# A 40-row product split over the two halves of TensorE's rows, in a linear-attention and mixture-of-experts kernel

## Chip, cores and metric

The kernel runs on one core of one Trainium2 chip, in fp32 (matmuls of the second part in fp32r). The metric is the time of one execution in device microseconds (us), as the core's own clock gives it. Full-speed TensorE clock is written 1.00; the profile shows which share of it was granted.

## What is computed

The first part is a recurrence over 768 tokens for 4 batches and 8 heads of width 40; its output feeds a mixture of 8 experts whose gate is normalized in 8 rounds over rows and columns.

```python
for t in range(S):                       # S = 768, state is [B, H, 40, 40]
    y[:, :, t] = einsum('bhd,bhde->bhe', rt, state)
    Sa = einsum('bhde,bhe->bhd', state, at)
    state_decay = state * wt[:, :, None, :] - einsum('bhd,bhe->bhde', Sa, bt)
    state = state_decay + einsum('bhd,bhe->bhde', vt, kt)
...
P = exp(logits - logits.max())           # logits = x @ w_gate, x = y as [3072, 320]
for _ in range(8):
    P /= P.sum(1, keepdims=True) + 1e-09
    P /= P.sum(0, keepdims=True) + 1e-09
    P *= N / E
for e in range(E):
    out += P[:, e:e + 1] * (maximum(x @ w1[e], 0.0) @ w2[e])
```

## The kernel before

**The recurrence in chunks.** The tokens are cut into 12 chunks of 64, and each chunk of each batch is one unit, 48 in all. A unit holds four pairs of heads (p, `NP` = 4). Of a pair, one head lies on partitions 0 to 39 and the other on 64 to 103 (`R2` = 104 rows); the rows between are padding. Three kinds of work make up the first part:

- **Preparations** (`prep`, 48 of them, numbered cb). One loads `inp` by DMA, forms the running products of the decays by two scans on VectorE (`q`, L124, and `g`, L134), scales k and b by `q` into `kb` (L147) and a by `g` into `ab` (L153, L154), and multiplies the two on TensorE into `ll` (L159): for each pair one product with the 128 columns of `kb` as weights. `ab` is laid out with 128 columns, of which the first head fills 0 to 63 in its rows and the second 64 to 127 in its own; the other two blocks were set to zero once at the start (L85), so that one product over all 104 rows gives both heads side by side. Then `kb` is transposed into `kt` (L167). `ll` goes to `sx` (VectorE, L169, with a mask) and to `lt` (ScalarE, L161 or L173), from which a DMA takes it to `ld` in DRAM; `kt` goes to `sx` and `bb` by three copies on ScalarE (L174 to L176). The first six preparations (`NFAST`) scale `ab` on VectorE, the others on GpSimd.
- **Inversions**: for every two chunks a triangular system is loaded back from `ld` (`load_lu`) and inverted in small steps on VectorE (L184 to L207), then assembled on TensorE and ScalarE (`tmat`: `gp`, L261, and `op`, L266, with weights of 64 rows by 64 columns).
- **Recurrence steps** (`recur`): `av`, `xc`, `pu`, `c2` and `zt` on TensorE, with evacuations on VectorE and ScalarE, and `y` (L321) and `z` (L330) on GpSimd. Spread between them are the gate's small products `lp` (L345).

**Buffers.** PSUM has eight banks: four for the recurrence steps (pool `ps`), two in pool `pq` and two in pool `pt`. `pq` holds `ll`, one bank each, and from preparation 6 on (`NKB` = 6) also `kt`; `pt` holds `gp`, `op`, `lp`, and `kt` of the first six. `kb`, `lt` and `q` have one buffer from preparation 6 on, `inp`, `g` and `ab` two.

**Order.** Events are sorted by hand-given times (`ev`), and a scheduler then places each engine's instructions by its own model of their lengths. Each engine works its queue in order. The second part (the experts, from L582 and L647) is dense TensorE work and follows the first.

## Time and profile before

| | us |
|---|---|
| median of 3 runs | 1834.67 (1831.1 to 1841.27) |
| the profiled execution | 1832.94, its span 1831.2 |
| TensorE busy over the span | 1724.3 (94%) |
| VectorE, ScalarE, GpSimd busy | 1365.3, 856.8, 874.0 |
| first and last `ll` product | 10.4 and 367.9 |
| last `op` product of the first part | 489.7 |

The first row is what a comparison goes by; the second is the execution whose trace is read here. Busy time of TensorE is counted from an instruction's start to its modelled end, and instructions overlap, so that 94% does not mean that no more would fit. The first part fills the first 500 us; all that the change touches lies in the first 371 us.

### The profile page before, as it was taken

Reading aid. Unit: us, or ns where it says so; the run is one execution under the profiler, and the core shown is the slowest. Engines: PE = TensorE matmul, PEld = TensorE weight load, DVE = VectorE, ACT = ScalarE, POOL = GpSimd, SP = SyncE. Lnnn points to the kernel's source line nnn. Section 1 sums busy time; section 2 is a strip of 40 time slices with the busy share of each in tenths; the row PEclk is TensorE's granted clock in tenths of the full one; section 3 lists DMA queues with packets and bytes.
Section 4 is the critical chain, followed back from the end, with each engine's and each line's share of the span. In section 5 each row is a group of like instructions: output and inputs, shape, how many; then the busy total and the mean of one; then the engine's idle time right before and its main releaser. Section 6 shows DMA issues by size and latency. Waiting matters only on the chain.

```text
span 1831.2 us, 31655 instructions
## 1 busy us (share of the span) xinstructions
PE 1724.3 (94%) x11843; PEld 1696.8 (93%) x11843; DVE 1365.3 (75%) x2356; ACT 856.8 (47%) x1851; POOL 874.0 (48%) x854
## 2 busy tenths in 40 slices
PE   4479988999989999999999999999999999999999
PEld 4368888898978999999999999999999999999999
DVE  7786996973788867777676878977686877767675
ACT  6347767766743533434343434345343343424342
POOL 6545664723462626447291735008182644628160
PEclk8568988999999999999999999999999999999999
DMA  7468777867520101111020112201020111102001
GB/s 193 116 157 185 175 180 174 186 137 172 152 77 20 57 20 57 38 39 57 20 75 20 57 37 61 69 1 60 16 76 20 57 38 38 57 20 75 15 24 44
DMA packets 211759, 140.47 MB, mean 77 GB/s; under 512 B 162965, under 2 KB 193813, under 8 KB 211605
## 3 DMA queue, kind: packets, MB, share of 16 engines
q1 hardware_dynamic: 207925, 132.70, 27.9%
q10 hardware_dynamic: 3680, 5.74, 1.2%
q8 instruction: 94, 1.54, 0.3%
q14 instruction: 60, 0.49, 0.1%
HBM read 110.78 MB, written 27.61 MB: 76 GB/s over the span
## 4 chain that ended last, share of the span: by engine, by line
PE 75%; DVE 7%; DMA 4%; issue 4%; POOL 3%; ACT 2%; SPq 2%; POOLq 0%; ACTq 0%; DVEq 0%
PE op L647 36%; PE p L582 33%; DMA inp<-in_inp_dram 1%; PE xc L297 1%; PE av L289 1%; PE pu L308 1%; DVE pr L193 1%; DVE hl L606 1%; DVE q L124 1%; PE c L315 1%; DMA ld<-lt 1%; PE op L266 1%; DVE sm L600 1%; PE ll L159 1%; POOL ab L154 1%
## 5 line engine op out<-in xcount | busy, mean ns | idle before, releaser
L582 PE MATMUL p<-xch,wh 128*128 128x384 f32 (+1 forms) x1792 | 605.0, 339 | 8.9 <-DVE sm L600 4.3
L603 ACT ACTIVATE hh<-sm 128x384 fp32r<-128x384 f32 x512 | 269.5, 527 | 728.5 <-DVE sm L600 728.4
L647 PE MATMUL op<-wh,hh 128*128 128x320 f32 x1536 | 477.2, 311 | 4.0 <-ACT hh L603 3.8
L647 PE MATMUL op<-wl,hh 128*128 128x320 f32 x1536 | 474.8, 310 | 0.0
L647 PE MATMUL op<-wh,hl 128*128 128x320 f32 x1536 | 468.0, 309 | 0.9 <-DVE hl L606 0.9
L528 POOL TENSOR_TENSOR wl<-ws,wh 128x640 fp32r<-128x640 f32 x60 | 103.1, 1718 | 606.2 <-ACT wh L526 606.1
L606 DVE SCALAR_TENSOR_TENSOR hl<-sm,hh 128x384 fp32r<-128x384 f32 x512 | 373.1, 762 | 2.6 <-ACT hh L603 1.8
L582 PEld LDWEIGHTS p<-xch,wh 128*128 128x128 f32 (+1 forms) x1792 | 337.0, 188 | 13.3 <-DVE sm L600 5.2
L582 PE MATMUL p<-xcl,wh 128*128 128x384 f32 x896 | 302.3, 337 | 0.0
L582 PE MATMUL p<-xch,wl 128*128 128x384 f32 x896 | 301.8, 337 | 0.0
L647 PEld LDWEIGHTS op<-wh,hh 128*128 128x128 f32 x1536 | 290.2, 189 | 4.9 <-ACT hh L603 4.9
L647 PEld LDWEIGHTS op<-wl,hh 128*128 128x128 f32 x1536 | 291.1, 190 | 0.0
L647 PEld LDWEIGHTS op<-wh,hl 128*128 128x128 f32 x1536 | 286.8, 188 | 1.4 <-DVE hl L606 1.2
L600 DVE TENSOR_TENSOR sm<-p,u 128x384 f32<-128x384 f32 x384 | 236.3, 625 | 8.7
L582 PEld LDWEIGHTS p<-xcl,wh 128*128 128x128 f32 x896 | 168.6, 188 | 0.0
L582 PEld LDWEIGHTS p<-xch,wl 128*128 128x128 f32 x896 | 168.5, 188 | 0.0
L600 DVE TENSOR_TENSOR sm<-p,p 128x384 f32<-128x384 f32 x128 | 71.3, 557 | 129.4 <-PE p L582 75.0
L600 DVE TENSOR_TENSOR p<-p,p 128x384 f32<-128x384 f32 x128 | 71.1, 556 | 101.7 <-PE p L582 101.4
L600 DVE TENSOR_TENSOR u<-p,p 128x384 f32<-128x384 f32 x128 | 70.8, 553 | 57.1 <-PE p L582 55.9
L536 POOL TENSOR_TENSOR wl<-ss,wh 128x512 fp32r<-128x512 f32 x60 | 90.3, 1505 | 28.4 <-ACT wh L533 24.2
L159 PE MATMUL ll<-ab,kb 104*128 104x128 f32 x336 | 62.8, 344 | 40.5 <-POOL kb L147 18.5
L159 PEld LDWEIGHTS ll<-ab,kb 104*128 104x128 f32 x336 | 54.2, 244 | 45.3 <-POOL kb L147 24.8
(163 smaller groups left out, 2727.3 us busy)
## 6 DMA issues: line engine op xcount, KB each, us to landing
ws<-in_wts_dram SPq DMA_DIRECT2D x60, 832.0 KB, 4.5
inp<-in_inp_dram SPq DMA_DIRECT2D x42, 451.5 KB, 4.5
gd<-g SPq DMA_DIRECT2D x48, 113.8 KB, 2.6
gl<-gd SPq DMA_DIRECT2D x48, 113.8 KB, 2.8
vz<-in_v_dram SPq DMA_DIRECT2D x48, 112.0 KB, 3.5
xd<-y SPq DMA_DIRECT2D x24, 224.0 KB, 3.5
ld<-lt ACTq DMA_DIRECT2D x40, 128.0 KB, 2.6
rb<-in_r_dram SPq DMA_DIRECT2D x96, 48.0 KB, 3.1
```

Of the source, the lines that this page charges most:

```text
L124: nc.vector.tensor_tensor_scan(out=qr.rearrange("r p t -> r (p t)"), data0=w65[:, 260:0:-1], data1=one65, initial=0.0, op0=ALU.mult, op1=A ...
L154: eng.tensor_tensor(out=ab[64:104, :, 64:128], in0=a_in[64:104], in1=g[64:104], op=ALU.mult)
L159: nc.tensor.matmul(ll[:, p], lhsT=kb[:, p], rhs=ab[:, p], start=True, stop=True)
L193: nc.vector.tensor_tensor(out=prv, in0=a.unsqueeze(2).broadcast_to([nu, n_c, n_r, n_k]), in1=m.unsqueeze(1).broadcast_to([nu, n_c, n_r, n_ ...
L266: nc.tensor.matmul(op[:, p], lhsT=gs[:, p], rhs=t2[:, p], start=True, stop=True)
L528: g.tensor_tensor(out=wl[:, 0:640], in0=raw[:, 256:896], in1=wh[:, 0:640], op=ALU.subtract)
L536: g.tensor_tensor(out=lv[:, 3:7], in0=so[:, :, 0], in1=hv[:, 3:7, 0], op=ALU.subtract)
L582: nc.tensor.matmul(o, lhsT=w_, rhs=x_, start=(j == 0), stop=(j == 3))
L600: eng.tensor_tensor(out=out, in0=x, in1=y, op=ALU.add)
L603: nc.scalar.activation(out=hh[:, f, h], in_=sm[f][:, h], func=AF.Relu)
L606: v.scalar_tensor_tensor(out=hl[:, f, h], in0=sm[f][:, h], scalar=0.0, in1=hh[:, f, h], op0=ALU.max, op1=ALU.subtract)
L647: nc.tensor.matmul(ops[i], lhsT=a[:, h, cs], rhs=w_[:, cw], start=(f == 0 and h == 0 and j == 0), stop=(last and h == 1 and j == 2))
```

## The change

The product of a preparation is taken for each head by itself: weights are the 40 rows of that head, moving data the 64 columns of its `ab`, so that the heads at rows 0 and 64 use different halves of TensorE's rows (two row tiles of 64). They write into different banks: `ll` is now one buffer of two banks, heads in one bank each, and `pq` has one such buffer (`PQ` = 1). `ab` loses its zero blocks and is filled by one operation over 104 rows in place of two over 40. `kt` of all preparations is now in `pt`.

```diff
-    ab_b = [pin.tile([R2, NP, 128], F32, name=f"ab{i}") for i in range(2)]
+    ab_b = [pin.tile([R2, NP, 64], F32, name=f"ab{i}") for i in range(2)]
...
-    for t in g1_b + ab_b:
+    for t in g1_b:
         nc.vector.memset(t, 0.0)
...
-        eng.tensor_tensor(out=ab[0:40, :, 0:64], in0=a_in[0:40], in1=g[0:40], op=ALU.mult)
-        eng.tensor_tensor(out=ab[64:104, :, 64:128], in0=a_in[64:104], in1=g[64:104], op=ALU.mult)
-        nc.scalar.copy(out=sx[64:104, :, 0, 0:64], in_=ab[0:40, :, 0:64])
-        nc.scalar.copy(out=sx[64:104, :, 1, 0:64], in_=ab[64:104, :, 64:128])
-        ll = pq.tile([128, NP, 2, 64], F32, name="ll", tag="pq")
+        eng.tensor_tensor(out=ab, in0=a_in[0:R2], in1=g[0:R2], op=ALU.mult)
+        nc.scalar.copy(out=sx[64:104, :, 0, 0:64], in_=ab[0:40])
+        nc.scalar.copy(out=sx[64:104, :, 1, 0:64], in_=ab[64:104])
+        lb = pq.tile([128, 2, 512], F32, name="ll", tag="pq")
         for p in range(NP):
-            nc.tensor.matmul(ll[:, p], lhsT=kb[:, p], rhs=ab[:, p], start=True, stop=True)
+            for h in range(2):
+                r = slice(h * 64, h * 64 + 40)
+                nc.tensor.matmul(lb[:, h, p * 64:p * 64 + 64], lhsT=kb[r, p].rearrange("r k t -> r (k t)"),
+                                 rhs=ab[r, p], start=True, stop=True)
+        ll = lb[:, :, 0:256].rearrange("x h (p t) -> x p h t", p=NP)
...
-            kt = pt.tile([128, NP, 2, 64], F32, name="kt", tag="pt")
-        else:
-            kt = pq.tile([128, NP, 2, 64], F32, name="kt", tag="pq")
+        kt = pt.tile([128, NP, 2, 64], F32, name="kt", tag="pt")
...
-PQ = 2
+PQ = 1
```

Lines below the edit stand one further down in the changed kernel (L167 becomes L168). The scheduler places the work anew. Three places show it. The first is TensorE's queue where the first inverse is assembled (`gp`, `op`), behind the preparations of the second group. Before:

```order
L159 MATMUL ll_1100<-ab1_222,kb_1090 128x128 x4
L167 MATMUL kt_1105<-cst_162,kb_1090 128x104 x4
L261 MATMUL gp_934<-td_219,lg_220 64x32 x8
L266 MATMUL op_945<-td_219,lg_220 64x32 x8
L261 MATMUL gp_1059<-td_219,lg_220 64x32 x8
L308 MATMUL pu_985<-x1_966,tt0_217 128x104 x4
```

In the changed kernel:

```order
L160 MATMUL ll_885<-ab1_222,kb_876 128x64 x8
L262 MATMUL gp_980<-td_219,lg_220 64x32 x8
L160 MATMUL ll_1059<-ab0_221,kb_1050 128x64 x8
L267 MATMUL op_991<-td_219,lg_220 64x32 x8
L168 MATMUL kt_1068<-cst_162,kb_1050 128x104 x4
L309 MATMUL pu_1031<-x1_1012,tt0_217 128x104 x4
```

A preparation's `ll` now stands between `gp` and `op`, its `kt` behind `op`, and the second `gp` comes after the next recurrence products; `kt`, `gp` and `op` draw on the same two banks.

The second place is GpSimd's queue in the preparations of the second group (the numbers name buffers). Before:

```order
L147 TENSOR_TENSOR kb_499<-st15_191,q_492 104x512
L152 COPY cc8_184<-q_581 104x4
L153 TENSOR_TENSOR ab0_221<-inp_579,g_584 40x4x64
L154 TENSOR_TENSOR ab0_221<-inp_579,g_584 40x4x64
L147 TENSOR_TENSOR kb_588<-inp_579,q_581 104x512
```

In the changed kernel:

```order
L147 TENSOR_TENSOR kb_518<-st15_191,q_511 104x512
L152 COPY cc8_184<-q_603 104x4
L153 TENSOR_TENSOR ab0_221<-inp_601,g_606 104x256
L147 TENSOR_TENSOR kb_610<-inp_601,q_603 104x512
```

One operation on `ab` stands between two on `kb`, in the same order otherwise.

The third place is VectorE's queue in the first 45 us, where `ll` of the first preparations is taken out of PSUM into `sx` (the buffer numbers are left out of `q` and `ll`). Before:

```order
L169 TENSOR_TENSOR sx_164<-ll,cst 64x8x64
L134 SCALAR_TENSOR_TENSOR g<-inp,g_223 112x260
L124 SCALAR_TENSOR_TENSOR q<-st_192,cst 112x260
L153 TENSOR_TENSOR ab_222<-inp,g 40x4x64
L154 TENSOR_TENSOR ab_222<-inp,g 40x4x64
L128 RECIPROCAL g_223<-q 112x4
L134 SCALAR_TENSOR_TENSOR g<-st_192,g_223 112x260
L169 TENSOR_TENSOR sx_167<-ll,cst 64x8x64
```

In the changed kernel:

```order
L170 TENSOR_TENSOR sx_164<-ll,cst 64x8x64
L128 RECIPROCAL g_223<-q 112x4
L153 TENSOR_TENSOR ab_222<-inp,g 104x256
L134 SCALAR_TENSOR_TENSOR g<-st_191,g_223 112x260
L170 TENSOR_TENSOR sx_167<-ll,cst 64x8x64
L170 TENSOR_TENSOR sx_170<-ll,cst 64x8x64
L170 TENSOR_TENSOR sx_173<-ll,cst 64x8x64
L170 TENSOR_TENSOR sx_176<-ll,cst 64x8x64
```

The scans of the two preparations that follow have moved ahead of `sx_164`, and four masks of `ll` stand together, each of which now empties the only `ll` buffer before the next product may start.

## Prediction

> **What bounds the kernel now.** I read three views, in this order: busy time by stage, the chain of work that ended last, and single rows of the timeline. First the stages (columns: stretch, its length, busy us of TensorE, its weight loads, VectorE, ScalarE and GpSimd with counts, granted clock, DMA share, GB/s).

> ```profile
> 0.00:57.00 57.00, 28.94 (x142) 25.57 (x143) 38.17 (x67) 34.24 (x84) 38.07 (x66) 0.76 0.72 177
> 57.00:107.00 50.00, 21.66 (x96) 19.11 (x95) 42.92 (x71) 18.92 (x48) 29.97 (x32) 0.50 0.53 132
> 107.00:380.00 273.00, 245.63 (x2274) 235.38 (x2274) 215.72 (x379) 188.60 (x477) 150.76 (x176) 0.90 0.79 176
> 380.00:500.00 120.00, 114.99 (x1120) 109.99 (x1119) 74.95 (x136) 79.31 (x188) 43.88 (x53) 0.96 0.67 157
> 500.00:1831.00 1331.00, 1313.06 (x8217) 1306.75 (x8215) 993.58 (x1705) 535.70 (x1055) 611.28 (x528) 1.00 0.13 43
> ```

> From 500 us on TensorE is full (1313 of 1331 us) and nothing there is edited. Preparations run in the first three stretches. Up to 107 us no engine is full and TensorE runs at half clock for much of it; from 107 to 380 us TensorE is busy for 90%, VectorE for 79%. Which of them ends last is said by the chain of waits from 57 to 380 us, by line:

> ```profile
> by line: issue 16.9%; DMA inp<-in_inp_dram 8.0%; DVE pr L193 4.8%; DVE q L124 3.9%; DMA ld<-lt 3.9%; PE ll L159 3.8%; POOL ab L154 3.5%; POOL ab L153 3.2%; DMA lu<-ld 3.2%; POOL kb L147 3.0%; DVE gt L196 2.9%; DVE g L134 2.9%; POOL y L321 2
> ```

> It is spread thin: the loads of `inp`, the scans, the inversion and GpSimd's scaling all take turns. The two `ab` operations hold 6.7% of 323 us, 21.6 us; the product `ll` 3.8%, 12.3 us. These are the two terms that the change can move most.

> **The product on two halves.** How one instruction follows the next on TensorE at full clock (columns: start, length to the last modelled end, what, count; every fp32 product is recorded twice):

> ```profile
> 228.71 1.63 PE L297 MATMUL xc<-f,st 104*104 104x104 f32 x16
> 236.19 1.08 PE L159 MATMUL ll<-ab,kb 104*128 104x128 f32 x8
> 237.11 0.52 PE L167 MATMUL kt<-cst,kb 104*128 104x104 f32 x4
> 239.79 0.98 PE L345 MATMUL lp<-gs,y 104*128 104x8 f32 x8
> 240.63 1.14 PE L159 MATMUL ll<-ab,kb 104*128 104x128 f32 x8
> ```

> `ll` holds TensorE from 236.19 to the start of `kt` at 237.11: 0.92 us for 8 records, 0.115 each. `lp` has the same 128 weight columns but 8 moving columns instead of 128, and takes 0.84 for 8 records. So it is the weights that set the pace, and halving the moving columns gains nothing by itself. [...]

> The new product has 16 records with 128 weight columns each. All then hangs on whether the halves work side by side. The trace has one place where products on rows 0 to 63 (`gp`) and on rows 64 to 127 (`op`) wait in the queue together, at half clock:

> ```profile
> 110.40 1.91 PE L261 MATMUL gp<-td,lg 64*64 64x32 f32 x16 [0.73 <-DMA td<-nd]
> 114.25 1.59 PE L266 MATMUL op<-td,lg 64*64 64x32 f32 x13 [1.95 <-ACT lg L263]
> 115.56 0.31 PE L261 MATMUL gp<-td,lg 64*64 64x32 f32 x1
> 115.67 0.29 PE L266 MATMUL op<-td,lg 64*64 64x32 f32 x1
> 115.69 0.29 PE L261 MATMUL gp<-td,lg 64*64 64x32 f32 x1
> 115.77 0.29 PE L266 MATMUL op<-td,lg 64*64 64x32 f32 x1
> 115.80 0.29 PE L261 MATMUL gp<-td,lg 64*64 64x32 f32 x1
> ```

> Alone, `gp` goes at (1.91 - 0.29) / 15 = 0.108 us a record. Interleaved, `gp` still steps by 0.11 (115.69 to 115.80) and `op` by 0.10 (115.67 to 115.77): each half keeps its own pace. So eight records per half beside each other: 8 x 0.115 = 0.92 us. The densest row of records bounds how fast 16 can be issued:

> ```profile
> 230.08 0.26 PE L297 MATMUL xc<-f,st 104*104 104x104 f32 x1
> 230.27 0.30 PE L261 MATMUL gp<-td,lg 64*64 64x32 f32 x2
> 230.50 1.12 PE L289 MATMUL av<-rb,vz 104*104 104x128 f32 x8
> 234.70 1.11 PE L266 MATMUL op<-td,lg 64*64 64x32 f32 x16
> ```

> `op` goes at (1.11 - 0.22) / 15 = 0.059 (0.22 is the length of one), and 16 x 0.059 = 0.94 us. I take 0.94; the upper end is 16 x 0.115 = 1.84, the lower 0.92. The same rows price a change of tile size. `xc` steps by (1.63 - 0.26) / 15 = 0.09, but from its last record to `gp` it is 0.19: 0.10 more. The two `gp` records need 0.12, but `av` starts 0.23 later: 0.11 more. Together 0.21 us for going in and out, 0.4 at half clock. [...]

> So a preparation costs TensorE 0.94 + 0.21 - 0.92 = 0.23 us more at full clock, about 0.4 at half. For 31 preparations after 107 us that is 7.1 us, for the 8 from 57 to 107 us 3.2, in all 10.3. `ll` is busy for 56.9 us in this stretch (rows below) and 12.3 of them lie on the chain, a fifth; TensorE's queue is dense, so that a delay also pushes what is behind it. I take a third: **+3.4 us** (0 to +10.3).

> **One operation for `ab`.** Groups of the two stretches (busy us, mean ns, then idle time before and its releasers); the first two rows are those of 57 to 107 us, the others of 107 to 380:

> ```profile
> L159 PE MATMUL ll<-ab,kb 104*128 104x128 f32 x64 | 16.8, 441 | 28.3 <-POOL kb L147 15.5 <-POOL ab L154 12.8
> L154 POOL TENSOR_TENSOR ab<-inp,g 40x256 f32<-40x256 f32 x8 | 7.8, 972 | 0.6
> ...
> L159 PE MATMUL ll<-ab,kb 104*128 104x128 f32 x248 | 40.1, 310 | 6.9 <-POOL ab L154 4.6 <-POOL kb L147 2.2
> L147 POOL TENSOR_TENSOR kb<-inp,q 104x512 f32<-104x512 f32 x30 | 37.7, 1257 | 45.1 <-DVE q L124 30.6 <-PE kt L167 7.1 <-PE xc L297 6.1
> L154 POOL TENSOR_TENSOR ab<-inp,g 40x256 f32<-40x256 f32 x30 | 29.0, 968 | 2.3
> L153 POOL TENSOR_TENSOR ab<-inp,g 40x256 f32<-40x256 f32 x30 | 24.3, 809 | 21.5 <-DVE g L134 12.5 <-ACT c L304 2.5 <-ACT bb L176 2.4
> L124 DVE TENSOR_TENSOR_SCAN q<-inp,cst 112x260 f32<-112x260 f32 x30 | 24.1, 802 | 21.4 <-DMA inp<-in_inp_dram 17.5 <-POOL kb L147 3.1 <-POOL ab L154 0.7
> L321 POOL TENSOR_TENSOR y<-ws,gl 104x256 f32<-104x256 f32 x28 | 23.6, 842 | 29.9 <-DVE ws L317 27.2 <-issue 1.7 <-DVE g L128 0.2
> ```

> The pair costs (24.3 + 29.0) / 30 = 1.78 us. The one that takes its place has the shape of `y`, 104x256, which takes 0.84 in the same stretch: GpSimd's time follows the 256 elements of a row, not the rows. That saves 0.94 of 1.78, so at most 21.6 x 0.94 / 1.78 = 11.4 us of the chain. What is late next stands in the same rows: `kb` has waited 30.6 us for VectorE's `q`, and `q` 17.5 us for the load of `inp`, which an `ab` that is done sooner does not shorten where `kb` frees the buffer last. I take half: **-5.7 us** (0 to -11.4).

> **The start, to 57 us.** Gone are the zero blocks; and six `ab` pairs are single operations on VectorE:

> ```profile
> 1.19 1.03 DVE L85 MEMSET ab<- 104x512 f32 x2
> L153 DVE TENSOR_TENSOR ab<-st,g x4: 402/411/418, 9.4 to 26.8; 40x256 f32<-40x256 f32 x4
> L154 DVE TENSOR_TENSOR ab<-st,g x4: 423/423/1293, 9.9 to 27.2; 40x256 f32<-40x256 f32 x4
> L154 DVE TENSOR_TENSOR ab<-inp,g x2: 1295/1296/1296, 30.7 to 35.0; 40x256 f32<-40x256 f32 x2
> ```

> That is 1.03 us of memsets and six second operations of 0.42 to 1.30, 4.3 us with the medians; VectorE is busy for 38.2 of 57 us, so a part of the 5.3 shows: -1.5, between 0 and -5. Against it stands the single `ll` buffer: a product now waits for the mask of the one before. Such a turn is about 2.1 us of product at half clock and 0.7 of mask, and the four masks in a row make four turns; with two buffers product and mask overlapped by up to 0.7. I take +1.5 (0 to +4). Together **0** (-5 to +4).

> **`kt` in `pt`.** No row of before shows the 42 later `kt` beside `gp`, `op` and `lp`. Nearest is how long one holds its bank:

> ```profile
> 180.94 0.52 PE L167 MATMUL kt<-cst,kb 104*128 104x104 f32 x4
> 181.83 0.42 ACT L174 COPY sx<-kt 64x320 f32<-64x320 f32 x1
> 182.57 0.30 ACT L176 ACTIVATE bb<-kt 64x160 f32<-64x160 f32 x1
> ```

> From 180.94 to 182.87, 1.9 us; 31 of them hold 60 of the 546 bank-us of two banks in 273 us. That is little, but what waits for a bank waits at the head of TensorE's queue, and recurrence products stand behind it. If a quarter of each hold is waited for, 0.5 x 31 = 16 us. Below nothing: `ll` and `kt` no longer take turns in one pool, worth up to -2. I take **+2** (-2 to +16).

> **Sum**: +3.4 - 5.7 + 0 + 2 = -0.3 us on the profiled execution's 1832.9, so 1832.6; its own range, with the terms half way to their ends, 1825 to 1840. The profiled execution lies 1.7 us under the median of the three runs, inside their scatter. About 0.5%, 9 us, is what a measurement of this kernel can tell from no change.

> **Rivals.** *Faster, the shorter `ab` counts in full.* The chain gives the whole 11.4, the start 5, the extra time on TensorE hides in the 10% that it idles before 380 us: 1832.9 - 16.4 = 1816.5. For it: `ll` waited 28.3 us in 57 to 107 us, 12.8 of it for `ab`. Against: `q` and the loads are close behind. Chance 0.24. *Slower, the banks of `pt`.* `gp`, `op`, `lp` and `kt` wait for each other's evacuation at the head of TensorE's queue, 0.5 us per preparation: 1832.9 + 3.4 - 5.7 + 16 = 1846.6. It decides from 0.37 us per preparation on (31 x 0.37 = 11.5, which with the other terms is +9). For it: `ll` now stands between `gp` and `op`, with `kt` behind. Against: 60 of 546 bank-us. Chance 0.18. *The halves work in turn*, so that the change does not do what it says: 1.84 + 0.21 - 0.92 = 1.13 us more per preparation, 35 us for 31, and 2.1 at half clock, 17 for 8. Half of these 52, with -5.7 and +2: 1855. The interleaved rows speak against it; they have 64 weight columns, not 128. Chance 0.08.

> **How the numbers follow.** The forecast has 0.50, of which I give 0.04 to each side for the scheduler's new placement. Faster by over 0.5%: 0.24 + 0.04 = 0.28; slower: 0.18 + 0.08 + 0.04 = 0.30; within: 0.42. The range takes in the fast rival and the bank rival and leaves out most of the third: 1815 to 1851.

> **What would show it.** Records of `ll` that alternate between the halves about 0.06 us apart, and some 0.94 us from the first `ll` record to `kt`'s, plus a gap of 0.1 on either side: the product's term. One `ab` row of about 0.84 us on GpSimd, and `ab` under 12 us on the chain: the second. Rows of `gp`, `op`, `lp` or `kt` that wait for ScalarE's copies out of a `pt` bank: the fourth; more than 12 us of these and the forecast is wrong. `ll` of 2 us at full clock would prove the halves in turn.

## The result and the profile after

| kernel | median us | ratio to before, 95% interval |
|---|---|---|
| before | 1836.1 (1831.1 to 1841.27, 4 runs) | |
| changed | 1901.71 (1897.6 to 1906.08, 4 runs) | 1.0357 (1.0318 to 1.0397) |

The change costs 3.6%, some 66 us; the forecast was 1832.6 us, with a range that ended at 1851. The profiled execution took 1906.08 us, its span is 1904.2, 73.0 more than the span of the execution profiled before (each profile shows one execution, so this distance is not exactly that of the medians). Its stages, in the columns of the prediction's first view:

```profile
57.00:107.00 50.00, 21.17 (x150) 17.79 (x148) 39.92 (x68) 17.92 (x45) 18.22 (x23) 1.00 0.52 134
107.00:430.00 323.00, 289.56 (x2382) 272.00 (x2383) 215.07 (x373) 182.73 (x460) 114.74 (x145) 0.76 0.67 149
430.00:570.00 140.00, 135.09 (x1264) 129.08 (x1262) 75.96 (x142) 87.83 (x211) 44.05 (x56) 0.90 0.61 140
570.00:1904.00 1334.00, 1317.22 (x8233) 1311.53 (x8233) 990.50 (x1707) 536.44 (x1057) 610.97 (x528) 0.99 0.13 43
```

The same stretch of the kernel before:

```profile
107.00:430.00 323.00, 294.70 (x2770) 281.75 (x2771) 254.66 (x446) 219.48 (x556) 161.75 (x193) 0.91 0.77 171
```

The last stage does the work that filled 500 to 1831 us before, with TensorE busy for 1317 us against 1313, so almost nothing was lost there. In 323 us from 107 on TensorE issued 2382 records against 2770, and every engine and the DMA did less: less work got done, on a TensorE that was busy all the same, at a granted clock of 0.76 instead of 0.91. The 0.76 is too high and the 1.00 up to 107 us says nothing, since the trace after has no clock entry before 127 us and such a stretch is counted as 1.00; from 140 to 430 us, where both traces have entries, it is 0.74 against 0.93. A set of `ll` before 107 us takes 1.97 us, as at 311 us, where the granted clock is 0.50; at 186 us, where it is 1.00, it takes 1.11. So TensorE was at half clock here:

```profile
97.39 1.97 PE L160 MATMUL ll<-ab,kb 40*128 40x64 f32 x16
```

Where the loss builds up is seen at `pu`, one set of products per recurrence step. This view of the first step, before and after, gives count, duration (min, median, max in ns) and first and last start:

```profile
L308 PE MATMUL pu<-x,tt x8: 421/421/540, 117.4 to 119.0; 128*128 128x104 f32 x8
```

```profile
L309 PE MATMUL pu<-x,tt x8: 421/421/540, 120.1 to 121.7; 128*128 128x104 f32 x8
```

The twenty-seventh step, again before and after (the first start of each row):

```profile
L308 PE MATMUL pu<-x,tt x10: 275/275/336, 355.1 to 366.0; 128*128 128x104 f32 x10
```

```profile
L309 PE MATMUL pu<-x,tt x16: 275/275/275, 423.8 to 431.0; 128*128 128x104 f32 x16
```

The first step starts 2.7 us later, this one 69, and the distance stays between 63 and 72 us up to the last of the 48 steps. So all is lost between 120 and 425 us, where preparations and recurrence steps run beside each other.

The two parts that the change is about did on their engines what the prediction said. The product on TensorE at full clock (granted 1.00 from 186.0 to 187.2 us), first record of `ll` to first record of `kt`:

```profile
186.09 1.11 PE L160 MATMUL ll<-ab,kb 40*128 40x64 f32 x16
187.13 0.57 PE L168 MATMUL kt<-cst,kb 104*128 104x104 f32 x4
```

That is 1.04 us for 16 records: 0.94 and the 0.10 of a change of tile size. The halves run side by side: in turn, the prediction had 1.84. And `ab`, by line (busy us, mean ns, then idle time before and its releasers):

```profile
L153 POOL TENSOR_TENSOR ab<-inp,g 104x256 f32<-104x256 f32 x40 | 33.6, 839 | 50.7 <-issue 19.6 <-DVE g L134 8.4 <-DMA inp<-in_inp_dram 3.6
```

That is 0.84 us on the mean in place of 1.78, as was priced. In the chain of waits from 57 to 430 us `ab` has six pieces, 5.8 us in all (21.6 before):

```profile
171.54 0.68 POOL ab L153
...
393.29 0.69 POOL ab L153
```

What grew is waiting. The changed kernel's waits from 107 to 430 us (engine, line, what released it, us in total, times, longest):

```profile
POOL cc L152 <- DVE q L124: 62.2, 19, 9.2
DVE q L124 <- DMA inp<-in_inp_dram: 48.2, 9, 9.0
POOL st L152 <- DVE q L124: 19.8, 6, 9.0
PE ll L160 <- ACT lt L174: 6.2, 6, 2.3
PE gp L262 <- ACT bb L177: 1.9, 1, 1.9
```

Before, in the same stretch:

```profile
POOL kb L147 <- DVE q L124: 30.6, 4, 11.0
DVE q L124 <- DMA inp<-in_inp_dram: 17.5, 9, 5.6
POOL cc L152 <- DVE q L124: 16.6, 8, 6.8
```

The wait for `q` has moved from one GpSimd instruction to another, so all of GpSimd's rows for `q` have to be added up: 48.6 us before, 82.0 after. VectorE's wait for the load of `inp` went from 17.5 to 48.2. So GpSimd and VectorE wait longer for the next preparation's load and scan. TensorE itself waits for little, 34.6 us in all against 29.5 before: 6.2 of them for the single `ll` buffer, 1.9 for a bank of `pt`.

### The profile page after: what moved, and what is told of

It reads as the page before. It is cut to its first block, busy times and chain, and to the rows that moved or that the text cites. A ratio compares the mean times of both kernels' runs of the same rounds, so it can differ in the third digit from the quotient of the medians.

```text
span 1904.2 us, 32335 instructions
## 1 busy us (share of the span) xinstructions
PE 1794.0 (94%) x12227; PEld 1757.7 (92%) x12227; DVE 1351.6 (71%) x2348; ACT 858.0 (45%) x1851; POOL 820.0 (43%) x812
## 3 DMA queue, kind: packets, MB, share of 16 engines
q8 instruction: 97, 1.59, 0.3%
## 4 chain that ended last, share of the span: by engine, by line
PE 78%; DVE 10%; DMA 5%; SPq 3%; issue 2%; ACT 1%; POOL 1%; DVEq 0%; ACTq 0%; POOLq 0%
PE op L648 35%; PE p L583 32%; PE xc L298 3%; DVE pr L194 2%; PE av L290 2%; PE pu L309 1%; DMA inp<-in_inp_dram 1%; DMA rb<-in_r_dram 1%; PE ll L160 1%; PE c L316 1%; DVE gt L197 1%; PE gp L262 1%; DVE g L134 1%; DMA lu<-ld 1%; DVE q L124 1%
## 5 line engine op out<-in xcount | busy, mean ns | idle before, releaser
L322 POOL TENSOR_TENSOR y<-ws,gl 104x256 f32<-104x256 f32 x48 | 41.1, 857 | 158.9 <-DVE ws L318 110.4
L712 DVE SCALAR_TENSOR_TENSOR acc<-op,pmat,acc 128x320 f32<-128x320 f32 x168 | 91.2, 543 | 4.6 <-PE op L648 4.5
```

The lines of the kernel that those rows point to most:

```text
L322: nc.gpsimd.tensor_tensor(out=y[0:R2, :, b % 2], in0=ws[:, :, 0:64], in1=gl[0:R2, :, 0:64], op=ALU.mult)
L712: nc.vector.scalar_tensor_tensor(out=acc[:, m], in0=ops[i], scalar=pmat[:, n, e:e + 1], in1=acc[:, m], op0=ALU.mult, op1=ALU.add)
```

## Experiments

Eighteen kernels: sixteen that were timed, in the table, and two that run TensorE alone. The last column is the ratio less one, times 1836 us.

| run | ratio to before (95%) | us against before |
|---|---|---|
| `kt` in `pt` | 1.0021 (1.0003 to 1.0039) | +4 |
| ... and one `ll` buffer, old product | 1.0071 (1.0042 to 1.0099) | +13 |
| change, product over all rows | 1.0254 (1.0225 to 1.0282) | +47 |
| change, three `pt`, three `ps` | 1.0451 (1.0414 to 1.0487) | +83 |
| change, halves move 128 columns | 1.0155 (1.0120 to 1.0190) | +28 |
| before, `gp`/`op` move 64 columns | 0.9987 (0.9965 to 1.0009) | -2 |
| before, `ll` moves 64 columns | 1.0102 (1.0063 to 1.0141) | +19 |
| halves of 64 and 40 rows, 128 columns | 1.0196 (1.0175 to 1.0217) | +36 |
| ... with two `ab` operations | 1.0247 (1.0227 to 1.0267) | +45 |
| ... with `gp`/`op` moving 64 | 1.0117 (1.0093 to 1.0142) | +21 |
| control order, 40 rows, 64 columns | 1.0338 (1.0312 to 1.0363) | +62 |
| control order, 40 rows, 128 columns | 1.0330 (1.0293 to 1.0368) | +61 |
| control order, 64 and 40 rows, 64 columns | 1.0336 (1.0308 to 1.0363) | +62 |
| control order, 64 and 40 rows, 128 columns | 1.0314 (1.0287 to 1.0341) | +58 |
| halves in the order of the old product | 1.0059 (1.0037 to 1.0081) | +11 |
| old product in the control's order | 1.0267 (1.0224 to 1.0311) | +49 |

### The pools

From the kernel before, first only this, then also `PQ = 1`:

```diff
-        if cb < NKB: ...
-            kt = pt.tile([128, NP, 2, 64], F32, name="kt", tag="pt")
-        else:
-            kt = pq.tile([128, NP, 2, 64], F32, name="kt", tag="pq")
+        kt = pt.tile([128, NP, 2, 64], F32, name="kt", tag="pt")
```

> The kernel before, with kt of every preparation in pt (so the two one-bank buffers of pq hold ll alone). Theory A (a single ll buffer: the next ll waits at the head of TensorE's queue until ScalarE and VectorE have read the one before): the buffers of ll stay two, so 1825 to 1845 us. Theory B (kt in pt stands in the way of gp, op and lp): most of the loss, 1880 to 1905 us. Theory C (products on row halves cost TensorE its clock and its pace): there are none here, 1825 to 1845 us.

> The kernel before, with kt of every preparation in pt and pq cut to one one-bank buffer; its product over all 104 rows and its two ab operations stay. Theory A (single ll buffer): the whole loss, 1890 to 1915 us, with TensorE at half clock for over 130 us of the first part. Theory B (kt in pt): the same time as the run that moves only kt, if that is slow. Theory C (row halves): 1830 to 1850 us.

1839.53 and 1847.86 us: `kt` in `pt` costs 4 us, the loss of the second `ll` buffer 9, each with what its own new order did. Both pools together are 13 of the 66 us, so theories A and B fall as the main cause. Two runs from the side of the changed kernel; the first also keeps the zero blocks and the two `ab` operations:

```diff
-                r = slice(h * 64, h * 64 + 40)
-                nc.tensor.matmul(lb[:, h, p * 64:p * 64 + 64], lhsT=kb[r, p]..., rhs=ab[r, p], ...)
+                nc.tensor.matmul(lb[:, h, p * 64:p * 64 + 64], lhsT=kb[:, p]...,
+                                 rhs=ab[:, p, h * 64:h * 64 + 64], ...)
```

> The changed kernel, its pools and its two banks of ll, with each head's product taken over all 104 rows against a zero-blocked operand (eight products of 64 columns, no row halves) and two ab operations as before. Theory A (single ll buffer): 1895 to 1920 us, since the wait is as in the changed kernel and each product set is about 0.4 us longer. Theory C (row halves): 1835 to 1860 us.

```diff
-PC = 4
-PT = 2
+PC = 3
+PT = 3
```

> The changed kernel with three buffers of pt in place of two, and three of ps in place of four (eight banks in all, as before). Theory B (kt crowds pt): 1850 to 1880 us. Theory A (single ll buffer): that wait is untouched, 1895 to 1925 us, more if ps lacks its fourth buffer. Theory C (row halves): 1895 to 1925 us.

The first took 1883.72 us, between the theories: without row halves most of the loss is still there, but sixteen records on all rows take 1.8 us a set in place of 0.9 (0.110 each: 22.2 us for 202 records in the row from 479.20 us below), so it told less than was hoped. The second took 1916.77, which speaks against theory B once more, although the recurrence steps lost a bank in it too.

### The clock

The trace after shows TensorE at half clock for long stretches in which it is never idle for long: the longest goes from 307.9 to 331.8 us, with a granted clock of 0.51 and TensorE busy for all of its 23.9 us. So the next theory was that thin products hold the clock down.

> The changed kernel, with each half's product moving 128 columns (the head's 64 and 64 that nobody reads) in place of 64, so that as many columns move as weight columns are loaded. In the changed kernel's trace TensorE stays at half clock for up to 24 us in a row while it is never idle for long. Theory D (the clock comes up only after a stretch in which the products move about as many columns as they load, and a set of 64-column products breaks that stretch): time at half clock between 107 and 430 us falls from about 180 us to under 110, and the time to 1840 to 1865 us. Theory C (products on 40 rows of a half count as little work, however many columns they move): 1890 to 1920 us, with the same long stretches. Theory S (neither: the waits of a single ll buffer or the order of the work): 1890 to 1920 us.

> The kernel before, with gp and op moving 64 columns per 64 weight columns in place of 32 (the other 32 are not read). Each record is set by its weight load (58 ns), so TensorE's time for them should stay. Theory D: these sets no longer hold the clock down; time at half clock between 107 and 430 us falls from about 52 us to under 40, and the time to 1820 to 1833 us. Theories C and S: 1832 to 1842 us, the same within the measurement.

> The kernel before, its pools and its two ab operations, with ll moving 64 columns in place of 128: the second heads' half of the product is left out, and what reads it reads the first heads' in its place. Four products a set at the pace of their weight load, as before, on 104 rows, two buffers, no row halves. Theory D: longer stretches at half clock, over 100 us between 107 and 430 us, and 1855 to 1900 us although work is left out. Theories C and S: 1828 to 1840 us.

Their edits:

```diff
-                nc.tensor.matmul(lb[:, h, p * 64:p * 64 + 64], ..., rhs=ab[r, p], ...)
+                nc.tensor.matmul(lb[:, h, p * 128:p * 128 + 128], ..., rhs=ab[r, p:p + 2]..., ...)
...
-            nc.tensor.matmul(gp[:, p], lhsT=lb[:, p], rhs=t1[:, p], ...)
+            nc.tensor.matmul(gp[:, p], lhsT=lb[:, p], rhs=t1[:, p:p + 2]..., ...)
...
-            nc.tensor.matmul(ll[:, p], lhsT=kb[:, p], rhs=ab[:, p], ...)
+            nc.tensor.matmul(ll[:, p, 0], lhsT=kb[:, p], rhs=ab[:, p, 0:64], ...)
```

1865.99 us (36 won back), 1832.27 (no difference that can be told) and 1854.24 (19 lost, although the second heads' half of the product is left out). The first and the third lie about 1 us outside theory D's ranges and over 10 us outside those of the others, so theory D looked right; the second fits all. TensorE alone was to settle what the clock does:

> TensorE alone; all of the reference's work is left out. After a pause of about 8 us each: 100 products of each kind in a row, 20 us or more (104 rows by 128 weight columns moving 128; halves of 40 rows in turn moving 64, then 128; 104 rows moving 64; one half of 40 rows moving 128; 64 rows by 64 columns moving 32, then 64; 104 rows moving 8), then each thin kind behind the dense one without a pause, then sets of four in turn with eight dense products. Theory D: the kinds that move as many columns as they load (dense, halves moving 128, one half, 64 by 64 moving 64) come to clock 1.00 within 3 to 8 us, the kinds that move half as many (64 on 128, 32 on 64) or 8 stay at 0.50 throughout, and fall back to it within 10 us behind dense ones. Theory C: the kinds on 40 rows stay at 0.50 whatever they move, and 104 rows moving 64 come up. Theory S: all kinds come up within 8 us.

> TensorE alone; all of the reference's work is left out. Kinds of 100 products behind pauses. Theory W, with a threshold somewhere between 0.77 (40 and 40 rows moving 128, which stayed at half clock) and 1.0 (104 rows moving 128): halves of 64 and 40 rows moving 128 and halves of 64 and 64 come up within 8 us; 64 and 40 rows moving 64 (0.5), 80 rows moving 128 (0.77), 104 rows moving 96 (0.75) and 128 rows moving 64 (0.62) stay at half clock; 96 rows moving 128 (0.92) and 104 rows moving 112 (0.88) place the threshold; 104 rows by 40 and by 64 weight columns come up if weight columns don't count, and stay if they do. Behind dense products halves of 40 and 40 moving 128 keep the clock and one half of 40 rows loses it. Theory M: 80 and 96 rows and 64 and 40 rows behave alike.

Stages of the first of these (length, TensorE's busy time and records, and after three idle engines' columns the granted clock):

```profile
20.50:40.00 19.50, 19.50 (x175) 19.50 (x174) 0.00 (x0) 0.00 (x0) 0.00 (x0) 1.00 0.00 1
50.00:92.00 42.00, 42.00 (x396) 42.00 (x398) 0.00 (x0) 0.00 (x0) 0.00 (x0) 0.50 0.01 2
102.00:144.00 42.00, 42.00 (x394) 42.00 (x396) 0.00 (x0) 0.00 (x0) 0.00 (x0) 0.50 0.00 1
154.00:196.00 42.00, 41.96 (x197) 41.96 (x197) 0.00 (x0) 0.00 (x0) 0.00 (x0) 0.50 0.00 0
425.40:463.10 37.70, 37.70 (x401) 37.70 (x400) 0.00 (x0) 0.00 (x0) 0.00 (x0) 0.57 0.00 1
479.20:501.40 22.20, 22.20 (x202) 22.20 (x200) 0.00 (x0) 0.00 (x0) 0.00 (x0) 1.00 0.00 1
629.00:646.50 17.50, 17.50 (x188) 16.49 (x186) 0.00 (x0) 0.00 (x0) 0.00 (x0) 1.00 0.00 1
```

In order: dense products of 104 rows at full clock; halves of 40 rows moving 64, halves moving 128, and 104 rows moving 64 columns, each behind a pause, at 0.50 for 42 us though TensorE never rests; then, behind dense products, halves moving 64, which lose the clock (0.57 over 37.7 us), and 104 rows moving 64, which keep it (1.00 over 22.2 us). The last row is sets of four halves pairs and eight dense products at full clock. In the trace the halves of successive sets start at 631.56, 634.58 and 637.60 us, so 3.02 us a set, against 24 x 0.1117 = 2.68 for the 24 records of twelve dense ones. So a set of halves with its changes of tile size (the "drains" of two expectations) costs 0.34 us more than the old one; the prediction had 0.23. The second of these runs:

```profile
20.00:40.00 20.00, 20.00 (x356) 20.00 (x356) 0.00 (x0) 0.00 (x0) 0.00 (x0) 1.00 0.01 2
49.60:92.00 42.40, 42.40 (x398) 42.40 (x400) 0.00 (x0) 0.00 (x0) 0.00 (x0) 0.50 0.00 1
135.50:178.00 42.50, 42.50 (x199) 42.50 (x200) 0.00 (x0) 0.00 (x0) 0.00 (x0) 0.50 0.00 1
187.70:211.70 24.00, 24.00 (x199) 24.00 (x200) 0.00 (x0) 0.00 (x0) 0.00 (x0) 0.92 0.00 1
273.00:316.00 43.00, 42.73 (x200) 42.73 (x200) 0.00 (x0) 0.22 (x1) 0.00 (x0) 0.50 0.00 0
377.50:397.70 20.20, 20.20 (x200) 20.20 (x200) 0.00 (x0) 0.00 (x0) 0.00 (x0) 0.88 0.01 2
```

Halves of 64 and 40 rows moving 128 come up (1.00), moving 64 they don't (0.50); 80 rows moving 128 stay (0.50), 96 rows come up (0.92); 104 rows moving 112 columns stay (0.50); 104 rows moving 104, with 40 weight columns, come up (0.88). In the last pair it is not the product of rows and moving columns by itself that goes with the clock (104 x 104 is less than 104 x 112): with 40 weight columns a record takes 0.173 us from start to start at half clock (as the four `zt` of this shape do from 316.89 us in the changed kernel), with 128 it takes 0.213 (42.5 us for 200). From these numbers I estimate rows times moving columns per us at half clock: 63 thousand for the one that came up, 55 thousand for the one that stayed. That agrees with theory W; what the clock follows is not shown. Theory D had expected the halves moving 128 to come up, theory C the 104 rows moving 64, and both missed; theory W's forecasts for the clock held. Those for the time did not:

> The run with halves moving 128 columns (1866 us), with the first half's product taken over all 64 rows of its half (rows 40 to 63 hold zeros in both operands, so the result is the same). Theory W (the clock counts rows times moving columns: with 64 and 40 rows a set is as much work as the product over 104 rows, with 40 and 40 it is 0.77 of it): TensorE comes up sooner, 55 to 80 us at half clock between 107 and 430 us, and 1845 to 1858 us, near the 1848 us of the old product on the same pools. Theory M (only the moving columns count, and what is left of the loss is the order of the work or the drains): no change, 1860 to 1872 us.

> The run with halves of 64 and 40 rows, with ab written by two operations of 40 rows in place of one of 104. If one operation is worth what the prediction priced for it (up to 0.9 us of GpSimd for each of 40 preparations, half of it on the path): 3 to 10 us longer than that run. If GpSimd is no bound here: within 3 us of it.

> The run with halves of 64 and 40 rows, with gp and op moving 64 columns as well. Theory W: the sets of gp and op go from 0.31 to 0.61 of the dense product's work for each us, so less time at half clock, 2 to 10 us shorter than the run with halves of 64 and 40 rows. Theory M: within 3 us of it.

```diff
-                r = slice(h * 64, h * 64 + 40)
+                r = slice(h * 64, 64 + h * 40)
...
-        eng.tensor_tensor(out=ab[:, 0:NP], in0=a_in[0:R2], in1=g[0:R2], op=ALU.mult)
+        eng.tensor_tensor(out=ab[0:40, 0:NP], in0=a_in[0:40], in1=g[0:40], op=ALU.mult)
+        eng.tensor_tensor(out=ab[64:104, 0:NP], in0=a_in[64:104], in1=g[64:104], op=ALU.mult)
```

(the second edit, and `gp` and `op` as above, each on top of the first). 1870.77 us, where theory W had 1845 to 1858: as much work as the old product, and no gain at all on the run before it. Two `ab` operations took 9.5 us longer, `gp` and `op` with 64 columns 13 us less (theory W had 2 to 10). But each of these kernels had been scheduled anew, and those with and without the 24 rows differ in their order on every engine: none of these steps compares one thing.

### One order

So the order was held fixed: the scheduler runs on one and the same program, and the operands of `ll` are resized afterwards, instruction by instruction.

```diff
     with tile.TileContext(nc, schedule_with_timeline_sim=True) as tc:
         body(tc, d, out)
+    resize(nc)
...
+            ins[n] = copy.replace(
+                i, ins=(copy.replace(rhs, ap=[[rhs.ap[0][0], rows], [1, COLS]]),
+                        copy.replace(lhs, ap=[[lhs.ap[0][0], rows], list(lhs.ap[1])])),
+                outs=(copy.replace(o, ap=[list(o.ap[0]), [1, COLS]]),))
```

> Control: the changed kernel with 64 unused columns behind ab and the products' results spread over both banks; 40 rows and 64 columns for each half, as in the change. The next three have this kernel's order on every engine, instruction by instruction. Both theories: 1890 to 1912 us.

> The control's order; each half moves 128 columns on 40 rows. TensorE alone kept its clock in this product and did not come up in it. Theory W (the clock): 15 to 40 us shorter than the control. Theory S (the order): within 6 us of it.

> The control's order; 64 and 40 rows, 64 columns. TensorE alone kept its clock in this product too, and did not come up in it: half the work of the dense product. Theory W: 8 to 35 us shorter than the control, and not shorter than the run of 40 rows and 128 columns by more than 5 us. Theory S: within 6 us of the control.

> The control's order; 64 and 40 rows, 128 columns, as much work as the product over 104 rows, and TensorE alone came up in it. Theory W: the shortest of the four, 20 to 50 us shorter than the control. Theory S: within 6 us of the control.

1896.48, 1894.02, 1895.6 and 1892.37 us. Thin or dense, the product makes 4 us, inside the scatter. The clock did react, from 140 to 430 us; first the control, then 64 and 40 rows moving 128:

```profile
140.00:430.00 290.00, 269.55 (x2241) 253.73 (x2239) 199.71 (x348) 173.41 (x439) 111.89 (x138) 0.74 0.66 153
```

```profile
140.00:430.00 290.00, 259.72 (x2300) 241.05 (x2300) 203.61 (x359) 176.79 (x447) 110.48 (x140) 0.82 0.68 155
```

The granted clock rose from 0.74 to 0.82, and TensorE only idled more (259.72 us busy in place of 269.55). So over this step the clock wasn't the bound; no run in this order had the 0.93 of the kernel before. The last two runs crossed products and orders:

> The kernel with the old product on one buffer of ll (1848 us), order of every engine as there; after scheduling each product of 104 rows and 128 columns is split into the change's two halves of 40 rows and 64 columns in two banks, and the readers of ll read the two banks. ab stays two operations with zero blocks. Theory S (the order): 1848 to 1866 us, where up to 16 us are the change of tile size on both sides of 48 sets (0.34 us a set at full clock, from TensorE alone). Theory P (the product itself: its clock, its drains): 1880 to 1905 us.

> The control (1896 us), order of every engine as there; after scheduling each pair of halves becomes one product over all 104 rows moving 128 columns into one bank, and the readers of ll read that bank. ab is not blocked by zeros, so the two heads' sums run together and the output is not the reference's. No row halves and no change of tile size are left, and each set takes 0.90 us at full clock. Theory S: 1878 to 1898 us. Theory P: 1845 to 1865 us.

The first replaces each product of the run with one `ll` buffer by two halves behind the scheduler, the second each pair of the control by one product, in which the two heads' sums run together:

```diff
+                for h in range(2):
+                    new.append(copy.replace(i, ..., tile_size=(64, 128), tile_position=(h * 64, 0), ...))
...
+                    held = copy.replace(i, tile_size=(128, 128), tile_position=(0, 0), ...)
```

| | order of the old product | order of the control |
|---|---|---|
| product over 104 rows | 1847.86 (+13) | 1884.9 (+49) |
| two halves | 1845.75 (+11) | 1896.48 (+62) |

Theory S holds on both sides (1845.75 lies 2 us under its range, 1884.9 inside it). The two kernels of the second column have the same order throughout, those of the first up to 486 us, where the experts begin to mix in. With the changed kernel's own product, the other order takes 51 us off (1.0338 against 1.0059); with the old product the control's order still costs 36. What the halves cost is -2 us in one order and +13 in the other. From 140 to 430 us the halves in the good order show a kernel like the one before, clock included (0.91, against 0.93 before and 0.74 for the same halves in the control), so thin halves by themselves do not hold it down here:

```profile
140.00:430.00 290.00, 271.71 (x2727) 257.47 (x2725) 223.23 (x391) 201.10 (x508) 149.69 (x179) 0.91 0.76 173
```

Where the bad order waits is seen in the DMA queue's own waits. SyncE issues nearly all loads and stores (in the control 342 of 375 from 107 to 430 us), one after the other, and an issue that waits holds all behind it: in the changed kernel the store of `g` (L138) waits 4.2 us for VectorE, SyncE issues nothing between 135.81 and 140.14 us, and the next load of `inp` goes at 142.52. From 107 to 430 us, halves in the good order (line numbers differ by two between these kernels):

```profile
SPq L277 <- POOL y L320: 8.7, 8, 2.7
SPq L138 <- DVE g L134: 7.9, 8, 2.7
```

The control:

```profile
SPq L138 <- DVE g L134: 28.8, 14, 5.6
SPq L279 <- POOL y L322: 21.8, 11, 5.0
SPq L381 <- DMA ld<-lt: 11.3, 6, 4.7
SPq L281 <- PE xc L298: 11.0, 5, 5.1
```

Storing a preparation's `g`, loading a recurrence's `gl` and the rest stand longer at the queue's head. All rows of this view add up to 81 us in the kernel before and 80 with the halves in the good order, and to 119 in the control, 115 with the old product in the control's order and 123 in the changed kernel. Over all the kernels this sum goes with the time: 74 to 81 us in those of 1848 us or less, 96 to 97 in those of 1854 to 1866, 105 to 111 from 1871 to 1884, 115 to 123 from 1885 on. That the two go together does not say which drives the other. Behind the waiting issues come the loads of `inp`, for which the scan `q` waits, and GpSimd's `cc` for `q`. The waits of all engines in the same stretch, first with the halves in the good order, then in the control:

```profile
POOL cc L152 <- DVE q L124: 18.3, 10, 3.8
...
DVE q L124 <- DMA inp<-in_inp_dram: 11.8, 8, 3.0
```

```profile
POOL cc L152 <- DVE q L124: 55.8, 17, 9.9
...
DVE q L124 <- DMA inp<-in_inp_dram: 43.3, 9, 9.8
```

GpSimd's rows for `q` add up to 33.6 us in the good order and 65.2 in the control.

On VectorE, the last 30 scans `q` stand behind 12.9 recurrence masks `pm` on the mean before, 12.8 in the good order and 12.0 in the control and the changed kernel: the preparations were put nearly one recurrence step earlier. A preparation in front of work that could have run, whose inputs are not there yet, would give these waits; that this is the mechanism is not shown. The count alone does not order the kernels: it is 12.5 in the run of 1857 us (`gp` and `op` moving 64) and in that of 1880 (two `ab` operations).

## Why the prediction was wrong

**The product on two halves: right in kind, the price too low.** +3.4 us with 0 to 10.3 was forecast from side-by-side halves and 0.23 us more a set. The halves do run side by side (1.04 us for 16 records), and a set costs 0.34 us more. Exchanged in a fixed order it was -2 us in one and +13 in the other, each with an interval of 7 to 9 us to either side; the +13, in an order nearly that of the change, lies above the forecast's upper end of 10.3, and its interval reaches down to 4.

**One operation for `ab`: right on the engine, not to be read in the time.** 0.84 us instead of 1.78, as priced, and 5.8 us on the chain instead of 21.6. GpSimd then waited more for `q`, as the row quoted there hinted ("`kb` has waited 30.6 us for VectorE's `q`"). Two operations instead of one took 9.5 us more, but with an order of their own.

**The start and the single `ll` buffer: mis-sized.** The first recurrence step came 2.7 us later, within 0 (-5 to +4). But +1.5 was priced for the first 57 us alone, and the buffer was left out after that; over the whole kernel it is 9 us (1.0021 to 1.0071), with the new order of that run.

**`kt` in `pt`: right.** +2 was forecast, 4 measured (0.5 to 7). The rival of the banks needed more than 12 us of TensorE waiting for them; 1.9 us was found.

**The step that failed** is the sum itself: each edit was priced on the order of the kernel before, and the new order got "0.04 to each side for the scheduler's new placement", a chance and no term in us. That placement is most of the result: 36 us with the old product and 51 with the halves, out of 66. From the kernel before to the changed one the runs make four steps: 13 for the pools, 36 for the order, 13 for the halves in it, and 3.5 from the control to the changed kernel (1.0338 against 1.0357, inside the scatter). They add up by construction, and the 13 of the pools hold whatever their own new order did. The first excerpt of the order that stood ahead of the prediction showed `ll` moved ahead of other work on TensorE, and I read it for its banks and not for what then stood behind a preparation that wasn't ready. A rival of that kind, with 30 to 60 us, was missing. The granted clock, which was in the first view, was priced nowhere. What was tested of it, 0.74 to 0.82 in the control's order, was worth 4 us; and the same halves ran at 0.91 in the good order, so the low clock followed from the order.

The sum's own range is wrong too: with the terms half way to their ends it goes from 1824 to 1848 us, not from 1825 to 1840. The range that was given in the end, 1815 to 1851, came from the rivals and does not hang on it.

What stays open: which of the moved instructions matters most, and what in the change made the scheduler move them. All kernels scheduled with eight products a set came out at +21 us or more, those with four at +19 or less, which is a hint and no proof. The order of the control was only run with one `ab` operation and the good order only with two; one operation in the good order wasn't tried. But the change's halves of 64 and 40 rows with two operations lost 45 us, and the product over all rows with two lost 47, so a loss of this size does not need the single operation. Nor was a kernel in the bad order given back its full clock.

## What to carry to other kernels

Where a scheduler places the work, a small edit can cost more through the new order than through anything that it does: give the placement a term of its own and bounds to match, and read the order excerpts for what stands behind an instruction whose inputs come late. To learn what an edit is worth, exchange it in a fixed order, both ways; of the ten runs here that were each scheduled anew, several told a story about the clock that did not hold once the order was fixed. A low granted clock beside idle neighbours need not be the reason for a loss: here the rise from 0.74 to 0.82 in a fixed order was worth 4 us, and the halves that ran at 0.74 in that order ran at 0.91 in the other.

## What the runs showed of the hardware

In the kernel before, from 226 to 246 us at a granted clock of 1.00, a change of tile size cost TensorE 0.10 and 0.11 us (the rows of the prediction). With TensorE alone at 1.00, a set of halves with both changes cost 0.34 us more than the same weights on all rows (3.02 against 2.68 us a set), although the halves' records run side by side (16 in 1.04 us in the changed kernel).
